# A spectral filter and a Fourier mixing layer on one core: a turn by DMAs or by TensorE, loads of x by halves or by groups, stores ordered or not

## The chip, the core and the metric

The kernel runs on one core of a Trainium2 chip. The metric is the device time in microseconds of one execution, median of several; shorter is better. A core has TensorE (matrix products; in the profile PE, its weight loads PEld), VectorE (DVE), ScalarE (ACT), GpSimd (POOL) and SyncE (SP), which here only issues loads. Each engine works through its own queue in order and waits on semaphores. 16 DMA engines move data between HBM and the on-chip memory SBUF, whatever engine issues the transfer. TensorE writes to PSUM, eight banks, from which ScalarE or VectorE must fetch the result.

## The reference

Two heads are computed from inputs of their own and set side by side.

```python
X = jnp.fft.rfft2(x_A, axes=(-2, -1))            # x_A: 1 x 2048 x 512
a = jnp.fft.irfft2(X * (w_r + 1j * w_i), s=(2048, 512), axes=(-2, -1))
p = jnp.einsum("bsd,ed->bse", x_B, dft_hid_re)   # x_B: 1 x 2048 x 512
q = jnp.einsum("bsd,ed->bse", x_B, dft_hid_im)
b = jnp.einsum("ts,bse->bte", dft_seq_re, p) - jnp.einsum("ts,bse->bte", dft_seq_im, q)
return jnp.concatenate([a, b], axis=-1)
```

Head A filters in the frequency domain. Head B is a two-dimensional Fourier transform, real part, whose transform matrices (2048 x 2048 and 512 x 512, cosine and sine) are inputs. All is float32.

## The kernel before, in words

The program is traced as named steps, and `PLAN` (lines 23 to 39) is the order in which they are written. Each step issues instructions on one engine or a few. Every instruction of TensorE, VectorE, ScalarE, GpSimd and SyncE goes through `_InOrder` (line 222), which pins it behind the one written before it on its engine; so each queue runs in the plan's order, and the profile shows the helper's line 229 for nearly all of them. They are told apart by tile names.

**Head A** splits the 2048 places of the sequence into 16 x 128.
- `forward(i)`, i = 0 to 7 (line 320): `xa` loads a slice of x transposed (tile `blk`), `fold` adds and subtracts its mirrored halves on VectorE (into `work`), `hid` applies the transform along the 512 channels (eight products of 256 columns, table `ta`, into a PSUM tile `pa`), `zs` copies to SBUF on ScalarE, `f16_` applies the 16-place transform (two products of 512 columns, the table f16 being the stationary operand), `ys` copies back. Then `tu` turns the data: two DMAs on POOL's queue write the result into eight partitions of the tile `zv` each, 16 DMAs in all, so that afterwards each partition holds one of 128 places.
- `slot(e, n)`, eight slots in the order `SLOTS` (line 386): `w` loads the filter's weights and a small table `fi`, `fix` (POOL) sets one column of the weights, `sf` (VectorE) folds z from `zv` into `work`, `fwd` is the 128-place transform (two products of 512 columns; slot 0 eight of 256), `prod` and `comb` multiply by the filter and combine on VectorE, `inv` transforms back (eight products of 128 columns), `ev` copies from PSUM to `zv` on ScalarE in two instructions. Slot 0, third in order, has special steps `g2`, `sx2`, `spec2`, `spy`.
- `inverse(j)` (line 513): `hi` is eight products of 256 columns that read `zv` with a stride as stationary operand, `eu` copies, `g16` is eight products of 128 columns, `sc` and `eo` add and subtract into `work`, and `st` stores 1 MB of out_a from POOL's queue after every second j. There are two places for what is stored; the third waits for the first one's store.

**Head B** uses that the given matrices are those of a Fourier transform, computes with small tables, and checks that they are.
- `xb` loads x by quarters (four tiles of 1 MB in the ring `blk`), each in two halves: rows going up on partitions 0 to 63 and rows going down on 64 to 127. The last half is loaded in three parts. `xr` reverses a part on ScalarE, `al` is four products on each of 16 groups (table `fb`), `av` copies to `yall`.
- `bh` is five products (table `bt`, with `yall` as stationary operand; the third has one row and 257 columns), `hv` copies to `zb`, `ro` is the product for one of eight blocks of rows. `y1`, `y2`, `y3` (ScalarE, VectorE, ScalarE) assemble 2 x 128 rows in a tile `yb`, of which there are two, and `pt` stores them from POOL's queue: a plain store (`out_b<-yb`) and an indirect one that writes the mirrored rows by an index table (`out_b<-yb,turn`). As both write the tensor out_b, each store waits for the one before it.
- The check: `cl` loads a block of the given matrices (1 MB, ring `blk`), `cc` compares it with a table `tt` on VectorE (SCALAR_TENSOR_TENSOR with a count of what differs); `sg` changes signs in the table on ScalarE. There are 34 blocks. If anything differs, a slow general path runs after the rest (it doesn't here).

The ring `blk` has six places of 1 MB for A's x, B's x and the matrices alike, given out in the order of the plan, and SP waits before a load until its place is free. PSUM has three tiles `pa` (head A, two banks each) and two `pb`.

Of the kernel before, what the change touches and what calls it, by code (L numbers as in the profile page):

```python
# [24 lines left out]
tu0 w1 f16_1 zs2 hid3 ys1 tu1 w2 cc0 f16_2 zs3 fold7 hid4 xb0 cc1 cl2 fix0 f16_3 zs4 ys2 hid5 tu2 xb1 cl3 fix1
ys3 tu3 f16_4 zs5 cl4 fix2 cl5 hid6 xr0 f16_5 zs6 cc2 al0 ys4 al1 av0 tu4 hid7 av1 cc3 f16_6 zs7 ys5 al2 sg4
tu5 f16_7 av2 cc4 al3 late cl6 av3 cc5 cl7 xr1 ys6 al4 ys7 tu6 al5 av4 tu7 al6 av5 cc6 al7 av6 cl8 av7 cl9 xb2
xb3 cc7 fwd2 sf0 sf1 tt2 cc8 cl10 cc9 fwd0 g2 fwd1 prod0 cl11 xr2 cl12 al8 prod1 w3 al9 cl13 av8 al10 av9
comb0 w4 al11 av10 av11 cl14 comb1 xr3 al12 sx2 al13 av12 cc10 al14 spec2 av13 inv0 av14 prod2 fix3 inv1 ev0
sf3 w5 al15 ev1 comb2 fwd3 cl15 av15 cl16 fix4 bh8 prod3 spy inv2 hv8 sf4 w6 fix5 comb3 fwd4 ev2 sf5 inv3  # L30
prod4 bh0 ev3 sf6 fix6 w7 fwd5 comb4 hv0 ro0 prod5 fix7 inv4 y10 y20 comb5 bh1 y30 ev4 rx sf7 hv1 fwd6 ry cc11
pt0 ro1 bh2 y11 prod6 cl17 sg12 inv5 hv2 y21 comb6 y31 ro2 ev5 pt1 bh3 y12 cc12 inv6 hv3 y22 cl18 fwd7 ev6
cc13 y32 ro3 pt2 bh4 prod7 y13 cl19 y23 hv4 comb7 ro4 y33 pt3 bh5 y14 cc14 inv7 hv5 y24 cl20 ev7 cc15 ro5 y34
bh6 y15 pt4 cc16 tt3 cl21 hi0 hv6 y25 cl22 sg17 y35 cc17 pt5 ro6 eu0 bh7 y16 tt4 cl23 y26 y36 g16_0 cc18 hv7
pt6 ro7 sc0 hi1 cc19 cl24 eo0 cl25 hi2 cc20 eu1 y17 y27 cl26 cc21 y37 g16_1 eu2 pt7 g16_2 cl27 sg22 sc1 cc22
hi3 sc2 eo1 cl28 eo2 st0 hi4 eu3 cc23 cc24 cl29 g16_3 eu4 g16_4 sc3 cc25 cl30 hi5 sc4 eo3 cl31 cc26 st1 hi6
eu5 cc27 cl32 eo4 cl33 eu6 cc28 g16_5 g16_6 sc5 cc29 hi7 sc6 eo5 sg30 cc30 st2 eu7 cc31 g16_7 eo6 sc7 eo7 cc32
st3 cc33
# [103 lines left out]
def _tables():  # L142
# [54 lines left out]
    for h in range(2):  # L197
        for kb in range(2):
            th = _ang(np.outer(_freqs(h), place[kb]), D)
            c, s = 2 * np.cos(th), -2 * np.sin(th)  # L200
            if h == 0:
# [18 lines left out]


class _InOrder:

    def __init__(self, tc, engine):
        self._tc, self._engine = tc, engine

    def __getattr__(self, name):
        def issue(*args, **kwargs):
            return self._tc.keep_in_program_order(getattr(self._engine, name)(*args, **kwargs))  # L229
# [4 lines left out]
def kernel(  # L234
# [85 lines left out]
    def forward(i):  # L320
        b, c = divmod(i, 2)
        zs = part(4096 + 1024 * (i % 2), 2, 512)
        ys = part(6144 + 1024 * (i % 2), 2, 512)
# [573 lines left out]
```

## Time and profile before

| | us |
|---|---|
| median of 3 runs | 258.09 (257.47 to 258.71) |
| the profiled execution, as timed | 258.96 |
| its span, first to last instruction | 257.2 |
| TensorE busy | 195.9 |
| VectorE busy | 154.0 |
| ScalarE busy | 71.9 |
| GpSimd busy | 39.3 |
| bytes moved | 70.35 MB, of these 57.54 read from HBM and 8.39 written |
| mean granted clock of TensorE | 0.856 of full speed |

Busy time of TensorE is modelled from pipelined products, so a full TensorE need not be at its peak. An idle time is printed with what ended it. The last instructions are the check's sum and its flag; after them the span holds 5.2 us without work.

### The profile page before, as it was taken

How to read it: one execution, taken by the hardware profiler on the slowest of the kernel's cores; microseconds unless marked ns; L12 is line 12 of the kernel's file. 1: busy time of each engine (PE TensorE's matmuls, PEld its weight loads, DVE VectorE, ACT ScalarE, POOL GpSimd, SP SyncE). 2: the span in 40 equal slices, each digit the busy share in tenths (PEclk: the TensorE clock that was granted, in tenths of full speed). 3: DMA queues.
4: the chain of work that ended last, by engine and by line, in shares of the span. 5: the costliest groups of instructions: out<-in, count | busy, mean ns of one | idle time of the engine just before them, and what ended most of it. 6: DMA issues, size and time to landing. Idle time of an engine off the chain costs nothing. (4 is left out here: it accounts for less than half of the span.)

```text
span 257.2 us, 2443 instructions
## 1 busy us (share of the span) xinstructions
PE 195.9 (76%) x857; PEld 153.9 (60%) x857; DVE 154.0 (60%) x209; ACT 71.9 (28%) x114; POOL 39.3 (15%) x55
## 2 busy tenths in 40 slices
PE   6799999397470798979999946994939999906800
PEld 1577776385470667948667623772718999906700
DVE  0730550031573789999999937814057799408990
ACT  1034150421720034531255402314031623300300
POOL 3002131012120000221013112010121120700110
PEclk9799999889677599999999985696577999965975
DMA  6989999999999999997314581786659889992440
GB/s 246 413 364 414 395 402 240 291 241 389 399 397 318 212 240 402 413 371 265 106 43 149 166 294 52 253 291 267 169 240 327 316 299 357 360 410 95 163 162 12
DMA packets 21746, 70.35 MB, mean 274 GB/s; under 512 B 2896, under 2 KB 3792, under 8 KB 20832
## 3 DMA queue, kind: packets, MB, share of 16 engines
q1 hardware_dynamic: 16656, 56.33, 63.8%
q0 software_dynamic: 4928, 13.22, 14.2%
q10 hardware_dynamic: 144, 0.59, 0.7%
q8 instruction: 8, 0.13, 0.2%
q14 instruction: 10, 0.08, 0.1%
HBM read 57.54 MB, written 8.39 MB: 256 GB/s over the span
## 5 line engine op out<-in xcount | busy, mean ns | idle before, releaser
L229 PE MATMUL pa<-ta,work 128*128 128x256 f32 (+1 forms) x256 | 48.8, 352 | 12.7 <-DVE work L229 11.5
L229 PEld LDWEIGHTS pa<-ta,work 128*128 128x128 f32 x256 | 43.3, 211 | 20.1 <-issue 10.2
L229 ACT COPY work<-pa 128x1024 f32<-128x1024 f32 (+3 forms) x36 | 30.4, 859 | 85.1 <-PE pa L229 82.9
L229 DVE SCALAR_TENSOR_TENSOR blk<-blk,tt 128x2048 f32<-128x2048 f32 (+2 forms) x24 | 41.6, 1756 | 20.3 <-DMA blk<-in_cm 17.4
L229 DVE SCALAR_TENSOR_TENSOR blk<-blk,odd,tt 128x2048 f32<-128x2048 f32 x16 | 37.5, 2346 | 21.7 <-DMA blk<-in_cm 21.7
L229 PE MATMUL pa<-ta,zv 128*128 128x256 f32 x128 | 31.0, 402 | 0.0
L229 PEld LDWEIGHTS pa<-ta,zv 128*128 128x128 f32 x128 | 29.7, 307 | 1.8 <-issue 1.0
L229 PE MATMUL pb<-bt,yall 128*128 128x257 f32 (+2 forms) x90 | 29.1, 459 | 0.0
L229 PEld LDWEIGHTS pb<-bt,yall 128*128 128x128 f32 (+1 forms) x90 | 18.0, 219 | 13.2 <-issue 11.7
L229 PE MATMUL pb<-fb,blk 128*128 128x200 f32 (+1 forms) x64 | 17.3, 358 | 8.3 <-ACT yall L229 4.4
L229 PE MATMUL pb<-zb,bt 128*128 128x512 f32 (+3 forms) x24 | 12.8, 641 | 13.8 <-ACT zb L229 13.8
L229 DVE TENSOR_TENSOR yb<-yb,pb 128x255 f32<-128x255 f32 x16 | 6.0, 415 | 26.4 <-ACT yb L229 26.4
L229 DVE TENSOR_TENSOR work<-work 128x512 f32<-128x512 f32 x32 | 20.6, 687 | 0.3
L229 PEld LDWEIGHTS pb<-fb,blk 128*128 128x128 f32 x64 | 13.2, 226 | 10.8 <-issue 5.9
L229 PE MATMUL pb<-fb,xr 128*128 128x200 f32 (+1 forms) x64 | 17.5, 359 | 2.1 <-ACT xr L229 2.1
L229 PEld LDWEIGHTS pa<-fi,work 128*128 128x128 f32 x144 | 18.6, 205 | 0.9 <-issue 0.5
L229 PE MATMUL pa<-fi,work 128*128 128x128 f32 x144 | 18.5, 288 | 0.0
L229 POOL DMA_INDIRECT out_b<-yb,turn x8 | 13.5, 1688 | 30.5 <-DMA out_b<-yb 16.9
L229 DVE TENSOR_TENSOR work<-pa,work 128x512 f32<-128x512 f32 x18 | 11.4, 682 | 11.2 <-DMA out_a<-work 11.2
L229 DVE TENSOR_TENSOR work<-pa,w 128x1024 f32<-128x1024 f32 x14 | 16.4, 1219 | 0.8 <-PE pa L229 0.8
L229 POOL DMA_DIRECT2D zv<-work x16 | 9.6, 605 | 46.8 <-ACT work L229 46.4
L229 ACT COPY yb<-pb 128x514 f32<-128x514 f32 (+1 forms) x9 | 5.1, 565 | 36.8 <-DMA out_b<-yb,turn 23.9
(48 smaller groups left out, 157.6 us busy)
## 6 DMA issues: line engine op xcount, KB each, us to landing
blk<-in_cm SPq DMA_DIRECT2D x32, 1024.0 KB, 10.7
tt<-tab_tt SPq DMA_DIRECT2D x4, 1026.0 KB, 10.5
w<-in_wa SPq DMA_DIRECT2D x8, 512.0 KB, 12.6
zv<-work POOLq DMA_DIRECT2D x16, 256.0 KB, 9.0
out_a<-work POOLq DMA_DIRECT2D x4, 1024.0 KB, 7.4
blk<-in_xb SPq DMA_DIRECT2D x7, 512.0 KB, 18.4
blk<-in_xa SPq DMA_DIRECT2D x4, 512.0 KB, 6.9
blk<-in_xa SPq DMA_DIRECT2D x2, 1024.0 KB, 11.0
```

Of the source, the lines that this page charges most:

```text
L229: return self._tc.keep_in_program_order(getattr(self._engine, name)(*args, **kwargs))
```

## The change

*A's turn.* `f16_` now takes the data as stationary operand, in eight pieces of 128 x 128, and the 16-place table as moving one: eight products of 128 columns in place of two of 512, with the result turned. `ys` writes it with a stride into a tile `fz`, so that the 128 places of a slot's rows lie in 128 consecutive columns. The step `tu` with its 16 DMAs is gone. Each slot gets two new steps instead: `tr` (eight, PE transposes of 128 x 128 against an identity matrix `eye`, which POOL loads at the start) and `ez` (ScalarE copies to SBUF, half of the result for seven slots, all of it for slot 0). `sf` reads one operand from PSUM and one from SBUF. `ev` is one copy, and `hi` reads `fz` with another stride. `fix` is now a copy on VectorE within `prod`. `m` in `work` has one place instead of two.

*x of B.* The load is by 16 groups of 64 + 64 rows, 256 KB each: one DMA for all 128 partitions of a group (three for the last), whose source has two runs of 64 rows as outermost dimension. `xr` still takes a quarter, four groups.

*out_b.* The stores are declared independent of each other. Every third block is assembled in `work` instead of in one of the two tiles `yb`, so three can be in flight.

*Besides.* `bh`'s third product takes every second column (128 instead of 257). The order of the queues is held by another means, which leaves out POOL: its instructions are ordered by the library's scheduler. `PLAN` is new throughout, and the numbers of the compared blocks (`cl`, `cc`, `sg`) have changed. The core of the diff:

```diff
-xa0 we xa1 xa2 xa3 xa5 xa7 tt0 tt1 bt fold0 cl0 fold1 hid0 cl1 fb fold3 hid1 zs0 w0 f16_0 zs1 fold5 hid2 ys0
...
+xa0 we xa1 xa2 xa3 xa5 xa7 cl0 cl1 fb fold0 hid0 bt fold1 tt0 cl2 fold3 hid1 zs0 cl3 tt1 f16_0 zs1 fold5 hid2
+ys0 cl4 f16_1 zs2 w0 hid3 ys1 f16_2 zs3 fold7 w1 hid4 ys2 cc0 xb0 cc1 f16_3 zs4 xb1 hid5 cc2 ys3 xb2 cc3 f16_4
+zs5 xb3 cc4 sg0 hid6 ys4 cl5 cl6 cl7 cl8 xb4 f16_5 zs6 xb5 xb6 hid7 xb7 xr0 ys5 cc5 f16_6 zs7 f16_7 w2 cc6 ys6
+al0 ys7 late cc7 al1 av0 tr0 av1 tr1 sg1 cc8 tr2 ez0 ez1 al2 sf0 al3 av2 sf1 fwd0 xb8 av3 xb9 xb10 xb11 cl9
+cl10 xr1 cl11 cl12 fwd1 prod0 ez2 fwd2 comb0 w3 prod1 tr3 g2 al4 ez3 al5 comb1 av4 w4 inv0 av5 sx2 al6 ev0 sf3
+al7 spec2 av6 cc9 cl13 inv1 av7 xr2 tr4 ev1 prod2 fwd3 ez4 comb2 al8 w5 al9 av8 al10 sf4 av9 spy al11 cc10
+av10 inv2 xb12 av11 xb13 xb14 xb15 cl14 prod3 cl15 fwd4 ev2 comb3 w6 tr5 xr3 tr6 prod4 ez5 al12 ez6 al13 av12
...
+st0 cc22 y36 pt6 cc23 cl28 ro7 eu2 hi3 y17 cc24 cl29 y27 g16_2 cl30 eu3 cc25 y37 g16_3 sc2 pt7 eo2 cl31 sg4
...
-    pe, dve, act, pool, sync = (_InOrder(tc, e) for e in (nc.tensor, nc.vector, nc.scalar, nc.gpsimd, nc.sync))
+    pe, dve, act, pool, sync = nc.tensor, nc.vector, nc.scalar, nc.gpsimd, nc.sync
...
+    written.enter_context(tc.manual_schedule(engines={e.engine for e in (pe, dve, act, sync)}))
...
-    zv = const("zv", 16, 512)
+    fz = const("fz", 4, 16, 128)
...
+    eye = const("eye", P, src=tabs["first"][:, 1152:], by=pool)
...
         @step(f"f16_{i}")
         def _():
-            y = flat(bank_a(("py", i)))
+            y = bank_a(("py", i)).rearrange("p r h q f -> p r (h q) f")
             for r in range(2):
-                mm(y[:, r], f16, zs[:, r], start=True, stop=True)
+                for c in range(4):
+                    mm(y[:, r, c], zs[:, r, 128 * c : 128 * c + 128], f16, start=True, stop=True)
...
-            act.copy(ys, flat(at["py", i]))
-
-        @step(f"tu{i}")
-        def _():
-            for r in range(2):
-                lo = _place(8 * r + i, 0)
-                pool.dma_start(zv[lo : lo + 29 : 4], ys[:, r])
+            act.copy(fz.rearrange("p c k (n g) -> p g (c k n)", g=16)[:, i::8], flat(at["py", i]))
...
-        m = part(3072 + 2048 * (n % 2), 2, 2, 4, 128)
+        m = part(3072, 2, 2, 4, 128)
+        z = part(5120 + (512 * (n % 2) if e else 0), 1 if e else 2, 2, 2, 128)
...
-        @step(f"fix{n}")
-        def _():
-            pool.tensor_copy(at["w", n][:, 0, :, :, 0], we[:, e].rearrange("p f r -> p r f"))
...
+        @step(f"tr{n}")
+        def _():
+            pz = bank_a(("pz", n)).rearrange("p r h q f -> p r (h q) f")
+            for r in range(2):
+                for c in range(4):
+                    pe.transpose(pz[:, r, c], fz[:, c, 2 * e + r], eye)
+
+        @step(f"ez{n}")
+        def _():
+            act.copy(z, at["pz", n][:, :1] if e else at["pz", n])
...
-                TT(out=t[:, :, 0], in0=z[:, 1], in1=z[:, 0, :, ::-1], op=ADD)
-                TT(out=t[:, :, 1], in0=z[:, 0], in1=z[:, 1, :, ::-1], op=SUB)
-                dve.tensor_copy(t[:, 0, :, :, 0], z[:, :, 0, :, 0])
+                pz = at["pz", n]
+                TT(out=t[:, :, 0], in0=pz[:, 1], in1=z[:, 0, :, ::-1], op=ADD)
+                TT(out=t[:, :, 1], in0=z[:, 0], in1=pz[:, 1, :, ::-1], op=SUB)
+                dve.tensor_copy(t[:, 0, :, :, 0], pz[:, :, 0, :, 0])
...
             x, w = at["px", n] if e else t, at["w", n]
+            dve.tensor_copy(w[:, 0, :, :, 0], we[:, e].rearrange("p f r -> p r f"))
...
-            for i in range(2):
-                act.copy(zv[:, 2 * e + i].rearrange("p (n q g) -> p n q g", n=8, q=4),
-                         at["pi", n][:, i].rearrange("p q h (n g) -> p n (q h) g", n=8))
+            act.copy(fz[:, :, 2 * e : 2 * e + 2].rearrange("p c k f -> p k c f"),
+                     at["pi", n].rearrange("p k h q f -> p k (h q) f"))
...
-                        mm(pu[:, k, h], gz[:, 32 * q + 16 * h + 2 * j + k :: 64], at["di"][:, h, q],
+                        mm(pu[:, k, h], gz[:, 2 * h + q, 2 * j + k], at["di"][:, h, q],
...
-            x = at["x", q] = block(("xb", q)).rearrange("p (g d) -> p g d", g=4)
-            lo = 16 + 256 * q
-            load(x[:64], src[lo : lo + 256].rearrange("(g r) d -> r g d", r=64))
-            lo = 16 * 124 - 256 * q - 192
-            if q < 3:
-                load(x[64:], src[lo : lo + 256].rearrange("(g r) d -> r g d", r=64)[:, ::-1])
...
+                if g == 0:
+                    at["x", q] = block(("xb", q)).rearrange("p (g d) -> p g d", g=4)
+                x, lo, low = at["x", q], 16 + 64 * n, 1984 - 64 * n
+                if n < 15:
+                    load(x[:, g], bass.AP(xb.tensor, lo * D, [[(low - lo) * D, 2], [D, 64], [1, D]]))
+                else:
+                    load(x[:64, g], src[lo : lo + 64])
+                    load(x[64:80, g], src[:16])
+                    load(x[80:, g], src[low + 16 : low + 64])
...
-            mm(out, yall[0:1, 9 + a1], hc[0:1, 1], start=False, stop=True)
+            mm(out[:, 1::2], yall[0:1, 9 + a1], hc[0:1, 1, 1::2], start=False, stop=True)
...
-            y = at["y", o] = sp.tile([P, 2, 512], F32, name="yb", bufs=2)
+            y = at["y", o] = sp.tile([P, 2, 512], F32, name="yb", bufs=2) if o % 3 < 2 else part(7168, 2, 512)
...
+                stores = [pool.dma_start(rows[8 * k, :64], y[64 * k : 64 * k + 64, 0]) for k in range(2)]
+            to = bass.IndirectOffsetOnAxis(ap=turn[:, o : o + 1], axis=0)
+            stores.append(pool.indirect_dma_start(out=out_b, out_offset=to, in_=y[:, 1], in_offset=None))
+            for i in stores:
+                tc.declare_no_dep(i.ins, group="rows", reason="every store has rows of its own")
+                tc.add_to_no_dep_group("rows", i.ins)
```

More of the change, by code (lines that the diff above doesn't have):

```diff
@@ L23 @@
 PLAN = """
-xa0 we xa1 xa2 xa3 xa5 xa7 tt0 tt1 bt fold0 cl0 fold1 hid0 cl1 fb fold3 hid1 zs0 w0 f16_0 zs1 fold5 hid2 ys0
[L25 to L38, printed above, removed]
+xa0 we xa1 xa2 xa3 xa5 xa7 cl0 cl1 fb fold0 hid0 bt fold1 tt0 cl2 fold3 hid1 zs0 cl3 tt1 f16_0 zs1 fold5 hid2
@@ new lines @@
+av10 inv2 xb12 av11 xb13 xb14 xb15 cl14 prod3 cl15 fwd4 ev2 comb3 w6 tr5 xr3 tr6 prod4 ez5 al12 ez6 al13 av12
+comb4 inv3 av13 sf5 al14 w7 ev3 al15 sf6 av14 inv4 av15 cc11 fwd5 ev4 cc12 cl16 tt2 fwd6 prod5 cl17 tr7 bh8
+ez7 comb5 bh0 hv8 prod6 inv5 hv0 ro0 comb6 ev5 bh1 y10 sf7 y20 inv6 hv1 cc13 y30 fwd7 ev6 cc14 cl18 cl19 rx
+ro1 ry prod7 y11 cl20 bh2 pt0 comb7 hv2 y21 inv7 cc15 y31 pt1 ro2 ev7 bh3 cc16 cl21 tt3 y12 hi0 hv3 y22 cl22
+sg2 y32 cc17 pt2 ro3 eu0 bh4 cl23 tt4 y13 y23 g16_0 y33 hv4 pt3 ro4 sc0 bh5 eo0 y14 y24 hi1 cc18 hv5 y34 pt4
@@ L206, in _tables @@
     first = np.concatenate([hf.reshape(2, 128, 512).transpose(1, 0, 2).reshape(128, 1024),
-                            f16.transpose(0, 1, 3, 2).reshape(128, 128)], 1)
+                            f16.reshape(128, 128), np.eye(128)], 1)
     late = np.concatenate([di.reshape(128, 1024), g16], 1)
@@ L483, in _ @@
         def _():
-            pi, it = bank_a(("pi", n)).rearrange("p r q h f -> p r (q h) f"), at["it", n]
+            pi, it = bank_a(("pi", n)).rearrange("p r h q f -> p r (h q) f"), at["it", n]
             for i in range(2):
                 for q in range(4):
-                    lhs = [yo[:, q % 2, k, q // 2] for k in range(2)]
+                    lhs = [yo[:, q // 2, k, q % 2] for k in range(2)]
                     if e:
@@ L681, in _ @@
             if o:
-                pool.dma_start(rows[o], y[:, 0])
+                stores = [pool.dma_start(rows[o], y[:, 0])]
             else:
-                for k in range(2):
-                    pool.dma_start(rows[8 * k, :64], y[64 * k : 64 * k + 64, 0])
-            pool.indirect_dma_start(out=out_b, out_offset=bass.IndirectOffsetOnAxis(ap=turn[:, o : o + 1], axis=0),
-                                    in_=y[:, 1], in_offset=None)
+                stores = [pool.dma_start(rows[8 * k, :64], y[64 * k : 64 * k + 64, 0]) for k in range(2)]
[4 more added lines that the diff above has]
+                tc.add_to_no_dep_group("rows", i.ins)
     for e in range(9):
@@ L760 @@
         table(k, q, mt)
-        for j in range(2 if q is None else 8):
-            if q is None:
-                compare_hidden(16 + j, j)
-            else:
-                i = 8 * k + j - (6 if k > 2 else 0)
-                compare(i, k, q, mt, *divmod(j, 4))
+        if q is None:
+            for h in range(2):
+                compare_hidden(16 + h, h)
+        else:
+            for j in range(8):
+                half, tb = divmod(j, 4)
+                compare(18 * q + 8 * half + 4 * mt + tb, k, q, mt, half, tb)
     for name in PLAN.split():
@@ L776 @@
     dve.tensor_scalar(flag, pf, 0.0, None, op0=ALU.is_equal)
+    written.close()
     first.close()
```

35 lines of the change are left out of this document (15 added, 20 removed).

## The prediction

> **What bounds the kernel now.** I read the totals first, then the stretches of the span, the chain of waits, the waits by engine, and the timeline around the two places that the chain pointed to.
>
> ```profile
> span 257.2 us, 2443 instructions
> PE 195.9 (76%) x857; PEld 153.9 (60%) x857; DVE 154.0 (60%) x209; ACT 71.9 (28%) x114; POOL 39.3 (15%) x55
> DMA packets 21746, 70.35 MB, mean 274 GB/s; under 512 B 2896, under 2 KB 3792, under 8 KB 20832
> ```
>
> No engine fills the span: TensorE has 61 us without work, VectorE 103. The time is in stretches with different limits (columns: stretch, its length, busy us of PE, PEld, DVE, ACT, POOL with instructions, granted clock, DMA share, GB/s):
>
> ```profile
> 0.00:43.60 43.60, 39.40 (x143) 27.99 (x144) 14.76 (x19) 11.31 (x11) 7.55 (x20) 0.96 0.96 356
> 43.60:93.40 49.80, 31.14 (x112) 24.52 (x111) 21.28 (x22) 13.40 (x22) 5.36 (x9) 0.79 1.05 312
> 93.40:150.00 56.60, 54.04 (x290) 40.67 (x289) 55.93 (x83) 22.98 (x46) 10.06 (x10) 1.00 0.69 244
> 150.00:200.00 50.00, 36.16 (x113) 26.44 (x113) 23.17 (x43) 11.29 (x20) 7.04 (x9) 0.69 0.66 236
> 200.00:222.50 22.50, 22.50 (x134) 22.45 (x134) 20.07 (x22) 8.02 (x10) 6.58 (x4) 1.00 0.90 331
> 222.50:233.00 10.50, 2.70 (x21) 2.48 (x19) 0.58 (x1) 1.60 (x2) 1.18 (x2) 0.73 0.99 378
> 233.00:252.00 19.00, 9.92 (x50) 9.38 (x50) 18.20 (x22) 3.33 (x4) 1.51 (x2) 0.77 0.30 115
> ```
>
> Up to 43.6 TensorE is the limit: A's hidden transform and 16-place transform follow each other without a gap. From 43.6 to 93.4 nothing computes fully while the DMA engines are full. From 93.4 to 150, A's slots keep VectorE at 99% and TensorE at 95%. From 150 on there are holes of 27 us (150 to 200) and 10 us (222.5 to 233) in VectorE. The first weak stretch in the timeline:
>
> ```profile
> 39.31 3.62 PE L229 MATMUL pa<-ta,work 128*128 128x256 f32 x16
> 42.77 1.88 PE L229 MATMUL pa<-work,ta 128*128 128x512 f32 x4
> 48.52 1.14 ACT L229 COPY xr<-blk 128x4 f32<-128x4 f32 x2 [9.65 <-DMA blk<-in_xb]
> 53.48 3.62 PE L229 MATMUL pa<-ta,work 128*128 128x256 f32 x16
> 68.47 1.94 ACT L229 COPY work<-pa 128x1024 f32<-128x1024 f32 x2
> 69.78 2.40 POOL L229 DMA_DIRECT2D zv<-work  x4 [7.20 <-ACT work L229]
> 85.13 6.46 PE L229 MATMUL pa<-zv,fi 128*128 128x256 f32 x16 [9.45 <-issue]
> 93.41 4.62 DVE L229 TENSOR_TENSOR work<-pa,w 128x1024 f32<-128x1024 f32 x4 [0.83 <-PE pa L229]
> ```
>
> Step hid6 starts at 39.31 and hid7 only at 53.48: ScalarE stands 9.65 us at xr0 for x of B, and zs6 behind it would have freed hid7's bank. Then the last two turns, tu6 and tu7, are issued at 69.78, and the first slot starts when they have landed, at 85.1. How transfers fared there:
>
> ```profile
> 20.00:30.00 10.00, 10.00 (x40) 7.33 (x39) 1.22 (x1) 3.04 (x3) 2.46 (x4) 1.00 1.02 407
> 80.00:90.00 10.00, 4.87 (x12) 3.91 (x13) 4.73 (x7) 0.00 (x0) 0.00 (x0) 0.52 1.07 230
> 90.00:100.00 10.00, 10.00 (x48) 7.58 (x46) 9.13 (x12) 3.34 (x7) 0.00 (x0) 0.96 1.04 296
> zv<-work POOLq DMA_DIRECT2D x16, 256.0 KB, 9.0
> blk<-in_xb SPq DMA_DIRECT2D x7, 512.0 KB, 18.4
> ```
>
> With equal DMA share (1.02 to 1.07) the engines moved 407 GB/s at 20 to 30 and 230 to 296 at 80 to 100, where the loads of x on 64 partitions lie. So these loads hold the engines without using them.
>
> The late holes, in the chain of waits and the waits by engine:
>
> ```profile
> 168.31 7.78 DMA out_b<-yb,turn
> 176.64 2.94 DMA out_b<-yb
> 180.35 8.08 DMA out_b<-yb,turn
> 222.14 10.18 DMA out_a<-work
> ACT yb L229 <- DMA out_b<-yb,turn: 23.9, 4, 9.2
> POOL out_b L229 <- DMA out_b<-yb: 16.9, 5, 5.5
> DVE yb L229 <- ACT yb L229: 26.4, 5, 8.9
> DVE work L229 <- DMA out_a<-work: 11.2, 1, 11.2
> ```
>
> The stores of out_b run one behind the other: a block's plain store, then its indirect one, then the next block's, 12.0 us a block (168.31 to 180.35). y1 waits for its buffer on ScalarE, y2 stands behind it on VectorE, and the compares, whose releases let SP load further blocks, stand behind y2.
>
> **The change, part by part.** Durations of the work it changes (the row with 4.66 is a stretch of TensorE's products with fb alone, four steps al; the row with slashes gives shortest, median and longest ns, first and last start):
>
> ```profile
> 120.41 1.95 PE L229 MATMUL pa<-fi,work 128*128 128x128 f32 x16
> L229 PE MATMUL pa<-work,ta 128*128 128x512 f32 x32 | 15.0, 593 | 0.0
> L229 ACT COPY zv<-pa 128x512 f32<-128x512 f32 x16 | 8.5, 585 | 9.5 <-PE pa L229 9.5
> L229 DVE COPY work<-zv 128x4 f32<-128x4 f32 x7 | 1.2, 171 | 0.2
> L229 PE MATMUL pb<-bt,yall 1*128 1x257 f32 x18 | 7.3, 490 | 0.0
> 94.86:99.52 4.66, 4.66 (x32) 4.66 (x32) 1.00 1.01 372
> L229 POOL DMA_INDIRECT out_b<-yb,turn x8: 1005/1326/2998, 135.7 to 219.1; - x8
> out_a<-work POOLq DMA_DIRECT2D x4, 1024.0 KB, 7.4
> SPq L229 <- DVE blk L229: 99.4, 22, 13.4
> ```
>
> *The 16-place transform* becomes eight products of 128 columns per i in place of two of 512. Eight products of that size with their weight loads took 1.95 us (inv, 120.41), against 1.88 us for the two: 8 x 0.07 = 0.6 us more, on TensorE's path.
>
> *The turn.* Sixteen DMAs of 256 KB go, with 4.2 MB of traffic and their wait: from the end of ys7 (70.4) to 85.1 it is 14.7 us. In their place stand 64 PE transposes and eight copies ez. No transpose is in this trace. The nearest row is the 128-column product, 1.95 / 8 = 0.24 us. The lower bound is half of it, if a transpose makes one pass where a product makes two (each product shows as two instructions); the upper is twice it, at half clock: 8, 16 or 31 us. I take 0.24, the row of the same shapes: 15.6 us, of which 5.9 lie before the first product. The Trainium skill, TensorE: Matmul & The Clock Gate, "Part 4: PE-mode transpose", gives some 275 ns for a bf16 transpose inside a kernel; by that figure the 64 would be an estimated 17.6 us and the sum 2 us more, and no run here shows it. The copies ez (0.59 us, 1.0 for slot 0) lie on ScalarE, 28% busy; only the first, 0.6 us, is on the path. ys writes with a stride: between 1.0 us as now and 2 us; up to 1 us on the path, since ScalarE has 5.4 us per i for two copies. ev loses one of two issues, nothing. sf reads one operand from PSUM; products of pa and w on the same engine do too, so I add nothing.
>
> *fix* goes from POOL to VectorE: 8 x 0.17 = 1.4 us on the path of the slots.
>
> *x by groups.* 18 issues on SP instead of 10, some 0.4 us each, 3 us, hidden under SP's 99 us of waiting for blocks; without that cover they are 3 us. If the groups move at the full 407 GB/s, the two stretches that held x lose their loss: 80 to 100 carried 5.3 MB where 8.1 would fit (7 us), 40 to 60 about as much. Behind SP's x loads are queued the cosine blocks, for which VectorE waits; behind xr on ScalarE everything that A needs there.
>
> *bh's third product* takes every second column: half of 7.3 us, 3.6 us off TensorE at most, 2 at full clock; I take 2. The eye load (64 KB, POOL) is long landed when tr0 starts.
>
> *out_b unordered, a third yb.* A buffer is held for about 2 us of y1 to y3, the issues, and 8 us of landing, 12 us; with three, one block per 4 us can go. TensorE's pace per block (bh and ro) is slower than that where hi and g16 lie between, so the wait goes. POOL is no longer held in written order, and st0 stands before pt6 and pt7 in the new order, so the 11.2 us wait for out_a's buffer shrinks; I leave 3 us of it.
>
> **The sum.** The slots' first product stands at 93.41 now. In the new order TensorE's chain sets it: f16_0 follows hid1 at 17 us as now and ends at 19, then six pairs of hid and f16 at 5.5 us (33 us), f16_7 to 54, ys7 to 55.3, al0, al1, tr0 to tr2, al2, al3, fwd0 to 67. By then x0 is there: 15.4 MB are ahead of it in SP's order (4.2 of A, five cosine blocks 5.2, tables 4.6, w 1.3, by the sizes of the loads), at 0.4 MB/us from 2 us 41 us, landed at 45. So the first product comes at **67**, 26 us earlier.
>
> From there TensorE is the longest. Its busy time from 93.4 on is 54.0 + 36.2 + 22.5 + 2.7 + 9.9 = 125.3 us. Moved behind the point: al4 to al7, 4.7; fwd1 and fwd2 (two products of 512 and eight of 256, as f16 and hid above), 5.5; tr3 to tr7, 9.8; less 2 for bh: 143. Of it 36.2 us ran at a clock of 0.69, 2.7 at 0.73 and 9.9 at 0.77; at 1.0, as where TensorE has no holes, they would take up to 14 us less. I take 10.5: 132.5. TensorE's share in the dense stretch 93.4 to 150 was 95%, so 139.5 us: the last product ends at 206.5. VectorE from the same point has 118.0 us as now, one compare (2.3) and fix (1.4) more, 121.7, which fits beneath; DMA has 66 MB, 165 us at 0.4, which fits too. After the last product come eo and st3: 1.3 + 0.8 + 7.4 landing, about 10; 3 us for out_a's buffer: 219.5. The profiled execution lies 1.8 us above its span (258.96 to 257.2): 221.3 on its scale, where the median of the runs is 0.9 lower: **220**. Its own range is 209 to 232: transposes at half price (8 us less) and a clock of 1.0 throughout (3.5 less) give the low end; transposes at twice the price, of whose 15.6 us VectorE's work covers a part, the high one.
>
> **The rivals.**
>
> *A: a group of x moves on two DMA engines only; slower.* The new source has two runs of 64 rows as its outermost dimension. If the transfer is divided over the engines by that count, each of two engines gets 128 KB per group. At 407/16 = 25.4 GB/s that is 5.2 us per group and 77 us for fifteen, on engines whose equal share of the other 62 MB is already 152 us: 229 us at the least. Worse, all later loads queue behind: x0 to x3 end at 62, four cosine blocks at 2.6 us and x4 to x7 at 93, w2 and x8 to x11 at 117, four blocks, w and x12 to x15 at 152. Each xr holds ScalarE until then. After 152 TensorE still has al12 to al15, four slots' second half, bh, ro and all of hi and g16, some 92 us by the rows above (al 4.7, inv 9.8, tr 2, the wider products by their columns at hid's 3.62 us for 2048), at 95% 97; with 13 us of tail and out_a's buffer, and 0.9 to the median's scale, **263**. It decides from two engines up to about four (a group 2.6 us: 245). For it: the shape. Against: in this trace all loads on SP had 64 or 128 rows outermost, so it shows neither. The Trainium skill, DMA: Bandwidth & Descriptors, "Why a DMA increments its semaphore by 16 and not by 1", says that the slowest dimension of both sides sets the number of engines, the largest up to 16 that divides both, which here would be two. No row here shows it; by that rule this rival is the result.
>
> *B: TensorE runs slow.* If the holes between short transposes keep the clock at its mean of 0.86, 143 stays 143: 150.5 at 95%, 11 us more than above, **231**. For it: 0.69 to 0.79 wherever TensorE waited. The Trainium skill, TensorE: Matmul & The Clock Gate, says in the section named above that transposes do not release the clock gate as products do; no row here has one.
>
> *C: the stores still pace.* From the first indirect store at 135.7 to the end of the last one's issue at 222.1 it is 86.4 us. Starting 26 us earlier but at that pace, with the 35 us that lie behind it now: 231.2, **232** with what lies around the span. That the change doesn't do what it says lies here: an order kept by another semaphore, or by POOL's own. Against it: no store reads what another writes.
>
> **Chances.** The forecast has 0.43, A 0.36 (slower 0.31, within 0.5% 0.03, faster 0.02), B 0.12, C 0.07, others 0.02 divided evenly. Faster by over 0.5% (about what this measurement tells from nothing): 0.43 + 0.02 + 0.12 + 0.07 + 0.01 = 0.65; same 0.03; slower 0.32. The range goes from 209 to 269: it cuts a tenth of the forecast and a quarter of A.
>
> **What would show it.** First product at 67 and xr0 before 50; 230 to 296 GB/s at full DMA share gone; transposes of 0.24 us; no wait of ScalarE for out_b's stores over 3 us. It is wrong if a group of x lands later than 10 us after issue, if xr1 to xr3 wait, or if the late clock stays under 0.8.

## The result, and the profile after

The change made the kernel slower: 275.51 us (274.81 to 275.87) against 257.78 us (257.14 to 258.71) for the kernel before, measured beside it, a ratio of 1.068 with a 95% interval of 1.064 to 1.072. The forecast was 220 us; rival A had 263.

The totals of the changed kernel:

```profile
span 273.2 us, 2751 instructions
PE 188.9 (69%) x1017; PEld 161.7 (59%) x1017; DVE 156.3 (57%) x217; ACT 83.5 (31%) x114; POOL 22.5 (8%) x32
GB/s 253 406 409 410 421 370 57 82 302 282 89 85 51 178 50 52 115 294 371 324 51 52 228 247 102 176 379 4 324 193 343 421 379 380 419 420 420 387 55 117
```

TensorE has 7 us less to do than before and POOL 17 us less, and the span is 16 us longer. The last of the three lines gives the moved bytes in 40 slices: in the middle it falls again and again to 50 to 57 GB/s, and once to 4. The same in stretches of 10 us (columns as in the prediction's table of stretches; the second last is the share of 16 DMA engines):

```profile
20.00:30.00 10.00, 10.00 (x62) 9.17 (x62) 1.88 (x3) 5.57 (x4) 0.00 (x0) 1.00 1.01 411
100.00:110.00 10.00, 8.78 (x37) 7.61 (x38) 1.34 (x3) 2.39 (x4) 0.00 (x0) 0.68 0.14 52
140.00:150.00 10.00, 10.00 (x69) 9.08 (x68) 5.08 (x8) 3.73 (x9) 0.00 (x0) 0.98 0.14 52
```

A share of 0.14 of sixteen engines is 2.2 engines, and they move 52 GB/s: two engines at 26 GB/s each, with the other 14 as good as idle. The loads of x on SP's queue (shortest, median and longest ns, first and last start):

```profile
L581 SPq DMA_DIRECT2D blk<-in_xb x15: 543/5062/11112, 31.7 to 140.1; - x15
```

and in the kernel before:

```profile
L229 SPq DMA_DIRECT2D blk<-in_xb x10: 596/631/1758, 32.8 to 80.2; - x10
```

SP stands 5.06 us at a group in the median, which is as long as 256 KB take at 52 GB/s (262,144 bytes / 52 = 5.04 us). What that does to the loads behind it shows in the timeline of SP's queue, loads of one kind in a row put together:

```profile
31.73 15.76 SPq L581 DMA_DIRECT2D blk<-in_xb  x4
47.60 10.62 SPq L712 DMA_DIRECT2D blk<-in_cm  x4
58.32 25.18 SPq L581 DMA_DIRECT2D blk<-in_xb  x4
83.53 5.12 SPq L387 DMA_DIRECT2D w<-in_wa  x1
88.69 0.47 SPq L260 DMA_DIRECT2D fi<-tab_fi  x1
89.26 18.84 SPq L581 DMA_DIRECT2D blk<-in_xb  x4
```

The six rows add up to 76.0 of the 76.4 us from 31.7 to 108.1; short gaps between the loads of a row are in them (1.8 us in the first), and by the single issues SP stands for 73.6. The weights and tables for A's slots, which the plan puts between the groups, go out when the groups before them have been taken. Who waits for all this:

```profile
ACT xr L594 <- DMA blk<-in_xb: 47.5, 3, 19.1
DVE blk L700 <- DMA blk<-in_cm: 40.2, 4, 25.5
PE pa L423 <- DMA fi<-tab_fi: 20.1, 1, 20.1
PE pa L427 <- DMA fi<-tab_fi: 18.0, 1, 18.0
POOL out_b L681 <- ACT yb L663: 18.8, 5, 5.0
```

ScalarE waits 47.5 us for x (before it was 9.65 at xr0 and next to nothing later), and TensorE 20.1 for one small table of 128 KB and 18.0 for that of slot 0, 512 KB. VectorE's 40.2 for the matrices are no more than before (39.1). The last line answers to the stores of out_b: POOL now waits for the block to be assembled, and no engine waits for a store. The places in time:

```profile
65.04 0.20 ACT L594 COPY xr<-blk 128x4 f32<-128x4 f32 x1 [19.07 <-DMA blk<-in_xb]
81.53 2.35 DVE L458 TENSOR_TENSOR work<-pa,w 128x1024 f32<-128x1024 f32 x2 [1.44 <-PE pa L423]
98.72 0.20 ACT L594 COPY xr<-blk 128x4 f32<-128x4 f32 x1 [18.46 <-DMA blk<-in_xb]
125.32 0.20 ACT L594 COPY xr<-blk 128x4 f32<-128x4 f32 x1 [10.01 <-DMA blk<-in_xb]
163.07 0.20 ACT L594 COPY xr<-blk 128x4 f32<-128x4 f32 x1 [12.86 <-DMA fi<-tab_fi]
```

The four quarters of x are copied at 65, 99, 125 and 163, and the first product of slots stands at 81.5 instead of 67. The last row puts its wait down to a table, but releasers are inferred and `xr` reads nothing but x: with that row ScalarE's waits before xr are 60.4 us. After the last quarter the kernel runs as it was meant to:

```profile
81.50:163.00 81.50, 33.38 (x190) 27.58 (x189) 34.84 (x52) 13.41 (x26) 0.00 (x0) 0.72 0.53 168
200.00:262.00 62.00, 61.91 (x329) 55.80 (x328) 52.82 (x74) 25.28 (x38) 16.48 (x17) 0.98 0.93 365
```

From 81.5 to 163 TensorE worked 41% of the time, from 200 on 100% at a clock of 0.98.

### The profile page after: what moved, and what is told of

It is laid out like the page before. It is cut to its first block, busy times and chain, and to the rows that moved or that the text cites. A ratio compares the mean times of both kernels' runs of the same rounds, so it can differ in the third digit from the quotient of the medians.

```text
span 273.2 us, 2751 instructions
## 1 busy us (share of the span) xinstructions
PE 188.9 (69%) x1017; PEld 161.7 (59%) x1017; DVE 156.3 (57%) x217; ACT 83.5 (31%) x114; POOL 22.5 (8%) x32
## 2 busy tenths in 40 slices
DMA packets 19393, 66.24 MB, mean 242 GB/s; under 512 B 1550, under 2 KB 2446, under 8 KB 18478
## 4 chain that ended last, share of the span: by engine, by line
DMA 33%; PE 32%; SPq 21%; DVE 9%; ACT 2%; issue 1%; ACTq 0%; DVEq 0%
SPq L581 14%; PE pa L519 10%; DMA blk<-in_cm 8%; DMA fi<-tab_fi 8%; DMA w<-in_wa 7%; DMA blk<-in_xb 6%; PE pa L531 5%; SPq L712 4%; DMA blk<-in_xa 4%; PE pa L484 3%; DVE work L458 3%; DVE blk L700 2%; PE pa L427 2%; PE pb L631 2%; PE pb L643 2%; SPq L387 2%
## 5 line engine op out<-in xcount | busy, mean ns | idle before, releaser
L346 PE MATMUL pa<-ta,work 128*128 128x256 f32 x128 | 31.5, 404 | 3.5 <-DVE work L334 3.5
L346 PEld LDWEIGHTS pa<-ta,work 128*128 128x128 f32 x128 | 25.6, 204 | 8.2 <-DVE work L334 4.4
L519 PE MATMUL pa<-ta,fz 128*128 128x256 f32 x128 | 29.5, 386 | 0.0
L519 PEld LDWEIGHTS pa<-ta,fz 128*128 128x128 f32 x128 | 28.9, 305 | 0.4 <-issue 0.2
L358 PE MATMUL pa<-ta,work 128*128 128x128 f32 x128 | 17.3, 293 | 17.0 <-ACT work L351 17.0
L423 PE MATMUL pa<-work,fi 128*128 128x512 f32 x28 | 14.4, 652 | 20.1 <-DMA fi<-tab_fi 20.1
L358 PEld LDWEIGHTS pa<-ta,work 128*128 128x128 f32 x128 | 17.0, 209 | 17.5 <-ACT work L351 17.2
L606 PE MATMUL pb<-fb,xr 128*128 128x200 f32 (+1 forms) x64 | 15.8, 330 | 11.3 <-ACT xr L595 11.3
L423 PEld LDWEIGHTS pa<-work,fi 128*128 128x128 f32 x28 | 5.4, 209 | 25.2 <-DVE work L416 20.3
L594 ACT COPY xr<-blk 128x4 f32<-128x4 f32 x4 | 0.8, 198 | 60.4 <-DMA blk<-in_xb 47.5
L606 PEld LDWEIGHTS pb<-fb,xr 128*128 128x128 f32 x64 | 11.5, 204 | 11.6 <-ACT xr L595 11.6
L362 ACT COPY fz<-pa 128x1024 f32<-128x1024 f32 x8 | 15.4, 1931 | 4.8 <-PE pa L358 4.8
L427 PEld LDWEIGHTS pa<-work,fi 128*128 128x128 f32 x16 | 4.7, 304 | 19.9 <-ACT work L408 18.8
L531 PEld LDWEIGHTS pa<-ta,work 128*128 128x128 f32 x128 | 15.1, 192 | 0.2
L351 ACT COPY work<-pa 128x1024 f32<-128x1024 f32 x8 | 8.1, 1018 | 22.9 <-PE pa L346 22.9
```

Of the source, the lines that this page charges most:

```text
L346: mm(pd[:, r, h], us(b)[:, h, c, k, 128 * r : 128 * r + 128], hf[:, k, h], start=k == 0, stop=k == 1)
L358: mm(y[:, r, c], zs[:, r, 128 * c : 128 * c + 128], f16, start=True, stop=True)
L362: act.copy(fz.rearrange("p c k (n g) -> p g (c k n)", g=16)[:, i::8], flat(at["py", i]))
L423: mm(flat(px[:, h]), ft[:, 0], flat(t[:, h]), start=True, stop=True)
L427: mm(px[:, h, i], ft[:, 2 * i + j], z[:, j, h], start=j == 0, stop=j == 1)
L519: mm(pu[:, k, h], gz[:, 2 * h + q, 2 * j + k], at["di"][:, h, q], start=q == 0, stop=q == 1)
```

## The experiments

Each run had runs of the kernel before beside it, whose medians were 256.7 to 259.5 us. "Laid out" means that the host puts the rows of x into the groups' order before the launch; that is no version for a user whose x comes in its own order, and its cost on the host is not in the time. All times are medians in us.

| kernel | time | ratio to before (interval) |
|---|---|---|
| before, with the two-run groups of x | 314.4 | 1.224 (1.217 to 1.231) |
| the change | 275.5 | 1.068 (1.064 to 1.072) |
| before, x laid out | 247.9 | 0.953 (0.945 to 0.962) |
| the change, groups with 4 outermost | 243.0 | 0.940 (0.930 to 0.950) |
| the change, groups by POOL's queue | 235.3 | 0.906 (0.899 to 0.913) |
| before, stores unordered | 226.4 | 0.878 (0.871 to 0.886) |
| the change, groups with 8 outermost | 220.7 | 0.855 (0.847 to 0.863) |
| the change, one group in four with two runs | 220.3 | 0.853 (0.848 to 0.857) |
| the change, x laid out, stores ordered | 218.1 | 0.845 (0.837 to 0.853) |
| before, x laid out, stores unordered | 215.9 | 0.830 (0.824 to 0.836) |
| the change, each group as two loads | 209.7 | 0.809 (0.801 to 0.817) |
| the change, x laid out | 205.3 | 0.796 (0.788 to 0.803) |

**Theory: a group of x moves on two engines, since two runs are the outermost dimension of its source, and everything behind it is late. Rival: the groups are a symptom; the new order, the transposes or the clock cost the time.** The first two runs take the two-run source away: once by laying out the rows, so that 128 rows are outermost, and once by two loads of 64 rows.

```diff
-load(x[:, g], bass.AP(xb.tensor, lo * D, [[(low - lo) * D, 2], [D, 64], [1, D]]))
+load(x[:, g], xg[:, n])
```

> The changed kernel with one thing else: the rows of x of B lie in HBM in the order in which the groups want them (a second copy of the input in another layout), so that each group is one load whose source has 128 rows outermost, 256 KB as before, 16 loads in all. Nothing else differs. Theory 1 (two engines): the source with two runs of 64 rows was divided over two DMA engines, and that alone turned a gain into a loss; then no stretch has under 60 GB/s with SP issuing x, the waits of ScalarE for x (47.5 us) fall under 5 us, the first product of the slots stands at 65 to 75 us instead of 81.5, and the time is 220, between 212 and 230. Rival (the new order and the work on TensorE and ScalarE cost the time, the loads are only where it shows): 255 to 275.

Measured: 204.9 us (204.3 to 206.1). Here the laid-out rows came in another order than the groups need, so its out_b was that of permuted rows; loads and instructions are the same. With the right rows:

```diff
+rows_b = np.concatenate([16 + 64 * np.arange(16) + np.arange(64)[:, None], low + np.arange(64)[:, None]])
+rows_b[64:80, 15] = np.arange(16)
+xg = xb.reshape(2048, 512)[rows_b]
```

> As the run with the laid-out rows, but with the rows taken in the order that the groups of the reference's sum need (in the earlier run they were taken from the input in another order, so its out_b was that of permuted rows; sizes and transfers were the same). The time should not see it: 205, between 203 and 208.

Measured: 205.3 us (204.1 to 206.9). Nothing but these loads was changed, their shape and the place of their rows (the three loads of the last group are one here), and 70.2 us went. The loads on SP's queue in this kernel:

```profile
L581 SPq DMA_DIRECT2D blk<-in_xg x16: 327/374/1983, 31.3 to 82.6; - x16
```

SP is held 0.37 us for a group instead of 5.06 (medians). The rival falls: the order and the transposes are the same here, and the clock went from 0.857 to 0.961 by itself once the holes were gone.

```diff
-load(x[:, g], bass.AP(xb.tensor, lo * D, [[(low - lo) * D, 2], [D, 64], [1, D]]))
+load(x[:64, g], src[lo : lo + 64])
+load(x[64:, g], src[low : low + 64])
```

> The changed kernel with each group of x loaded by two loads of 64 partitions instead of one of 128 (33 issues on SP instead of 18). Theory 1: every load has 64 rows outermost and goes over all engines, at the reduced rate that the kernel before had for 64 partitions (230 to 296 GB/s); 4 MB of that cost at most 10 us against the laid-out rows, most of it hidden: 220 to 234. Rival (SP's many issues are what holds the queue, 5 us each): with nearly twice the issues it is no faster than the changed kernel, 270 to 290.

Measured: 209.7 us (206.8 to 210.8), a ratio of 0.809 to the kernel before, with x as the user has it and nearly twice the loads: 65.8 us less than with one load a group. Laid-out rows have 0.796. The Trainium skill, DMA: Bandwidth & Descriptors, "Rules for kernel authors", advises one load of 128 partitions over two to disjoint halves. The medians of these two runs differ that way, by 4.4 us, but the intervals of their ratios overlap, so the runs don't settle it; and the merged load of the change is one load of 128 partitions as well.

**The groups alone, on the kernel before.**

```diff
-            load(x[:64], src[lo : lo + 256].rearrange("(g r) d -> r g d", r=64))
...
+            for g in range(4):
...
+                    load(x[:, g], bass.AP(xb.tensor, lo * D, [[(low - lo) * D, 2], [D, 64], [1, D]]))
```

> The kernel before with the new load of x alone: four groups, each one load whose source has two runs of 64 rows, in place of two loads of 64 partitions per quarter; order, turn by DMAs and ordered stores as before. Theory 1: each group takes some 5 us on two engines and SP, 16 of them; the four quarters' xr come 15 to 40 us later than before, and the time is 280, between 270 and 300. Rival (the damage is in the new order): 255 to 262.

Measured: 314.4 us (313.5 to 315.2), 57.6 more than the kernel before beside it.

```profile
L229 SPq DMA_DIRECT2D blk<-in_xb x18: 414/5088/8583, 32.8 to 144.5; - x18
```

SP's 5.09 us a group stand here too, with none of the rest of the change. So this part does the harm by itself; the rest of the change takes 38.9 us off again (314.4 to 275.5).

**Does the count of the outermost dimension set the number of engines?** The laid-out rows are padded, so that the source has 4 or 8 blocks outermost with the rest of the kernel as in the run with x laid out; the eight-block kernel has `[[272*D, 8], [16 * D, 16], [1, D]]`.

```diff
-load(x[:, g], xg[:, n])
+load(x[:, g], bass.AP(xg.tensor, n * D, [[528*D, 4], [16 * D, 32], [1, D]]))
```

> The laid-out rows, but stored in four runs of 32 rows with a gap behind each, so that the source of a group has 4 as its outermost dimension; same bytes, same number of loads, right rows. If the outermost count sets the number of DMA engines, a group takes 64 KB on each of four engines, 2.6 us at the 25 GB/s an engine had; SP's issue of a group takes about 2.5 us instead of 5; the four engines carry 40 us of x besides their share of the rest, and the time is 216, between 210 and 232. If only the two far runs of the changed kernel were special, it is 205.

> The same with eight runs of 16 rows. By the count: 32 KB on each of eight engines, 1.3 us a group, an issue about 1.3 us; nearly all hidden: 207, between 204 and 212, and not above the run with four. If the count means nothing, 205.

Measured: 243.0 us (241.1 to 243.3) and 220.7 us (220.2 to 221.1), both slower than expected. With four blocks, SP's queue, and a stretch in which SP issues only groups of x:

```profile
L581 SPq DMA_DIRECT2D blk<-in_xg x16: 529/2344/6946, 31.6 to 111.9; - x16
```

```profile
60.00:64.00 4.00, 3.76 (x17) 3.76 (x18) 3.70 (x5) 2.04 (x2) 0.00 (x0) 0.50 0.25 102
```

A share of 0.25 is four engines, at 25.5 GB/s each. So for two and four blocks the count is the number of engines, and SP's 2.34 us follow the 2.57 us that a group takes at 102 GB/s. With eight blocks SP is held 0.63 us, half of what the expectation had:

```profile
L581 SPq DMA_DIRECT2D blk<-in_xg x16: 596/633/3537, 31.9 to 95.5; - x16
```

The Trainium skill's rule, cited in the prediction under A (DMA: Bandwidth & Descriptors, "Why a DMA increments its semaphore by 16 and not by 1"), agrees with the traces for two and four. For eight no stretch shows the engines of a group: in the one in the last section blocks of the matrices are under way as well.

The size was missed because I had let most of each group's time lie beside other transfers. Worked out afterwards without any such cover, each load costs what it takes longer than the 0.64 us of 256 KB at 407 GB/s: 15 x (5.04 - 0.64) = 66 us for two, 16 x (2.57 - 0.64) = 31 for four, and with half of 2.57 as an estimate, 16 x 0.64 = 10 for eight. Measured against 205.3 us: 70, 38 and 15, each 4 to 7 us more than the sum. So other transfers cover hardly any of a group's time; where the 4 to 7 us come from was not followed, and for eight the rate is not shown by a run.

**Is it the loads themselves, or SP's standing?** One group in four is loaded by two runs, the three behind it are laid out.

```diff
+if g == 0:
+    load(x[:, g], bass.AP(xb.tensor, lo * D, [[(low - lo) * D, 2], [D, 64], [1, D]]))
+else:
     load(x[:, g], xg[:, n])
```

> The changed kernel with laid-out rows for x, but the first group of each of the four quarters is loaded as in the changed kernel (outermost dimension two), so four of sixteen loads go to two engines, with three full loads behind each. Theory one, that SP is held only once the two engines' backlog is deep: a lone group is taken at 0.5 to 0.7 us and its 5 us of moving lie beside the full loads behind it, 205 to 213 us. Theory two, that every such group costs the kernel what it cost on average in the changed kernel, (275.5 - 205.3) / 15 = 4.7 us, wherever it stands: 219 to 229 us, with SP held about 5 us for each.

Measured: 220.3 us (219.3 to 220.4 in five executions; a sixth took 651.6 us, for a reason that is not on record), in the time of theory two, 15.0 us for four such groups (the sum above gives 4 x 4.4 = 17.6). But theory one was right on SP's row, and neither saw the next:

```profile
L582 SPq DMA_DIRECT2D blk<-in_xb x4: 532/738/3048, 31.4 to 92.1; - x4
L584 SPq DMA_DIRECT2D blk<-in_xg x12: 328/608/7673, 33.8 to 96.9; - x12
```

The two-run groups are taken at 0.74 us in the median (one at 3.05); it is at the laid-out groups behind them that SP stands, up to 7.67 us. So the load at which SP stands need not be the one with the two runs: a load with 128 rows outermost is held too when a two-run group went out before it. What part of the chip makes it wait is not in the records.

```diff
-load(x[:, g], bass.AP(xb.tensor, lo * D, [[(low - lo) * D, 2], [D, 64], [1, D]]))
+pool.dma_start(x[:, g], bass.AP(xb.tensor, lo * D, [[(low - lo) * D, 2], [D, 64], [1, D]]))
```

> The changed kernel, and its fifteen two-row group loads of x are issued by POOL's queue in place of SP's; the groups and their access patterns stay as they are. Theory one, that the harm is SP being held: SP was held 5 us by each group, so that the loads behind it started late. With POOL held instead, SP's other loads go out at 0.4 to 0.6 us each, the first product of slots comes near 67 us, and the time is 225 to 245 us; some of the loss stays, since each group still takes 5 us (256 KB at 52 GB/s). Theory two, that the harm is the two engines themselves: every other load is spread over all the engines and so has parts behind the groups on those two, whoever issues them. Then the windows stay near 52 GB/s while groups move, loads other than x land 15 us or more after their issue, and the time is 262 to 282 us.

Measured: 235.3 us (234.8 to 235.8). The time is theory one's, but the run doesn't tell the two theories apart, for POOL's queue moves the same source in another way. Its rows of queues (packets, MB, share of the DMA engines), with those of the changed kernel behind them:

```profile
q0 software_dynamic: 10576, 13.07, 19.4%
```

```profile
q0 software_dynamic: 2656, 9.08, 8.7%
```

The fifteen groups are 7920 packets there, 528 each, most of them small (8480 packets under 512 bytes in this kernel, 1550 in the changed one), and the engines are all busy (a stretch of 10 us of the kernel with POOL's groups):

```profile
50.00:60.00 10.00, 1.23 (x11) 1.03 (x10) 3.51 (x3) 0.00 (x0) 2.28 (x3) 0.67 1.05 268
```

Whether one group is spread over all the engines there, or the next group takes other ones, is not in the records. So the idle engines and most of SP's standing (up to 4.30 us at a block of the matrices is left) went away together; how much each alone would cost stays open. The first product came at 83 us, not at 67 as expected: the four groups of x's first quarter were issued from 30.3 to 33.6 and copied at 66.4.

```profile
30.31 3.24 POOL L581 DMA_DIRECT2D blk<-in_xb  x4 [26.61 <-DVE work L337]
blk<-in_xb POOLq DMA_DIRECT2D x15, 256.0 KB, 27.2
```

A group takes 27.2 us from issue to landing here, in the median; the later ones also went out late, since POOL waited for places in the ring.

**What the rest is worth.** Four runs set A's new turn, with the new order and all else that goes with it (the third buffer, bh's third product), against the order of the stores. Stores ordered in the changed kernel, stores unordered in the kernel before (two buffers `yb` there):

```diff
 # the change, x laid out, stores ordered
-for i in stores:
-    tc.declare_no_dep(i.ins, group="rows", reason="every store has rows of its own")
-    tc.add_to_no_dep_group("rows", i.ins)
```

> The laid-out rows with out_b's stores left in order as in the kernel before; three buffers as in the changed kernel. If the order of the stores is worth as much here as in the kernel before (30 us), 230 to 240, with ScalarE or GpSimd waiting for the indirect stores; if the third buffer and the new order of the steps hide it, 206 to 214.

> The kernel before with the stores of out_b declared independent, two buffers yb as before, all else unchanged. If the stores' order made the holes between 150 and 200 us (27 us in VectorE), the blocks of rows follow at 5 to 8 us instead of 12, ScalarE's waits for the indirect stores (23.9 us) fall under 10, and the time is 238, between 230 and 246. If the two buffers are the limit, or the holes belong to the cosine blocks that SP loads, it is 250 to 258.

```diff
 # before, x laid out (and, in the second kernel, those three lines added)
-            load(x[:64], src[lo : lo + 256].rearrange("(g r) d -> r g d", r=64))
...
+            for g in range(4):
+                load(x[:, g], xg[:, 4 * q + g])
```

> The kernel before, with x read by sixteen groups from rows laid out in the groups' order (128 rows outermost in each load), and nothing else changed. Theory: x was not on the path in the kernel before (the copies xr waited 0.5 us for it), so full-rate groups bring at most the 2 us of the earlier row group: 252 to 259 us, a ratio of 0.98 to 1.00. Rival: that finer groups of x also let the transforms along x start earlier and fill TensorE's idle time: 235 to 248 us.

> The kernel before with the laid-out groups of x, and with the stores of out_b declared independent and two buffers yb; A's turn stays with its DMAs and the moving data. Against the changed kernel with laid-out rows (205.3 us) it shows what A's new turn and the order that goes with it are worth. Theory, that the parts add: 226.4 us of the stores alone less 0 to 3 us for x, 222 to 228 us, so that the turn is worth 17 to 23 us. Rival, that x and the stores together do nearly all of it: 205 to 213 us, and the turn is worth less than 8 us.

Measured, all with x laid out:

| | stores ordered | stores unordered | |
|---|---|---|---|
| A's turn by DMAs, the old order | 247.9 | 215.9 | -32.0 |
| the change: A's turn by transposes, the new order | 218.1 | 205.3 | -12.7 |
| | -29.8 | -10.6 | |

Three of the four runs fit neither of the ranges that their expectation gave. Ordered stores in the changed kernel gave 218.1, between the two. Unordered stores in the kernel before gave 226.4 us, 30.3 less than the kernel before beside it, more than expected. Together with x laid out they gave 215.9, between the two ranges. x laid out alone gave 247.9, 11.6 less, at the edge of what the rival had; the expectation had left out the 9.65 us that ScalarE waits at xr0. The two parts add there (30.3 + 11.6 = 41.9, measured 259.5 - 215.9 = 43.6). Turn and stores don't add: each gives some 30 us alone, and both together 42.5. So they go in part for the same time; which part that is, these runs don't show. The waits with ordered stores in the changed kernel:

```profile
ACT yb L648 <- DMA out_b<-yb,turn: 15.6, 2, 9.2
POOL out_b L677 <- DMA out_b<-yb,turn: 14.0, 3, 6.0
DVE yb L654 <- ACT yb L648: 11.3, 3, 7.6
ACT work L648 <- DMA out_b<-work,turn: 5.6, 1, 5.6
```

That is the chain of the kernel before (y1 for its buffer, y2 behind it), 15.6 us and, for the third buffer in `work`, 5.6 instead of 23.9, in spite of three buffers. Why x at full rate helps the kernel before, first as it was and then with x laid out, in the same 20 us:

```profile
30.00:50.00 20.00, 15.51 (x59) 10.90 (x59) 5.63 (x6) 5.44 (x7) 2.95 (x7) 0.99 1.05 324
```

```profile
30.00:50.00 20.00, 20.00 (x86) 15.41 (x85) 7.07 (x7) 7.65 (x11) 4.14 (x9) 1.00 1.05 394
```

TensorE has no hole there any more: ScalarE's wait at xr0 is 4.5 us instead of 9.65, and TensorE's stock of work covers it. These are 4.5 of the 11.6 us; where the others come from was not followed, nor whether the rate or the finer groups bring them.

## Why the prediction was wrong

**The step that failed** is "x by groups": "some 0.4 us each, 3 us, hidden under SP's 99 us of waiting" and "if the groups move at the full 407 GB/s". A group took 5.06 us of SP in the median and moved at 52 GB/s. Neither number had a row for this shape, and the text said so; the forecast took the rows of loads with 64 or 128 rows outermost for it. What could have been read in advance was read: A names the outermost dimension, the two engines and the order of what comes late, and the rule that would make it the result. I gave it 0.36 because no row showed it. But no row spoke against it either, and the forecast's own number hung as much on an unseen shape. The runs leave A as it was put, and they price it by itself: 70 us.

**A's size** was 263 against 275.5. It had the quarters of x at 62, 93, 117 and 152; they were copied at 65.0, 98.7, 125.3 and 163.1. So the lateness against A grows by some 3 us with each quarter (3.0, 5.7, 8.3, 11.1), and that is the miss, not the work behind it: from 163.1 to the end of the span it is 110.1 us, where A had 97 and 13. That this fits to 0.1 us is luck; the last products end at 261.9, so it is 98.8 and 11.3. Ahead of the fourth quarter SP stands at blocks and weights that were issued behind the third one's groups:

```profile
108.20 8.30 SPq L712 DMA_DIRECT2D blk<-in_cm  x4
116.60 4.18 SPq L387 DMA_DIRECT2D w<-in_wa  x1
135.84 9.31 SPq L581 DMA_DIRECT2D blk<-in_xb  x3
```

A had let every transfer follow the one before it without a gap, and had no term for SP's standing at an issue. How much of the 11 us each of the two makes was not followed further.

**With x at full rate the forecast was 15 us too high,** below its own range of 209 to 232. The kernel with x laid out, its transposes, its first product and its last products:

```profile
54.82 2.78 PE L405 MATMUL pa<-eye,fz 128*128 128x128 f32 x24
61.70 2.36 DVE L459 TENSOR_TENSOR work<-pa,w 128x1024 f32<-128x1024 f32 x2 [0.83 <-PE pa L424]
66.67 1.04 PE L405 MATMUL pa<-eye,fz 128*128 128x128 f32 x8
187.31 3.73 PE L532 MATMUL pa<-ta,work 128*128 128x128 f32 x32
```

- First product: forecast 67, measured 61.7. Of the 5.3 us, 3.1 are the first 24 transposes (5.9 forecast, 2.78 measured); 1.4 us more lie ahead of them, for the last 16-place product ends at 52.6 where the sum had 54. The remainder was not followed.
- From there to the last product of TensorE: forecast 139.5, measured 129.3 (61.7 to 191.0). The transposes are the largest term: eight take 1.04 us, 0.13 each, at the lower bound of 0.12, and each shows as one instruction, not two. I had taken the middle. For the 64 it is 7 us, 4.6 of them in this stretch (40 x 0.24 = 9.8, 40 x 0.13 = 5.2). Another 3.5 us would be the clock, if the 0.99 of the row under "The rivals" holds for the whole stretch: the sum had taken 10.5 of up to 14 us for a clock of 1.0.
- The tail: forecast 13 with 3 for out_a's buffer, measured 11.0 (191.0 to 202.0). No row of waits shows VectorE behind out_a's store any more. The three come to 17.5 us of the span; by the medians of the runs it is 15, since the profiled execution is the shortest of five.

**A duration at its upper bound, and off the path.** The strided ys, in the changed kernel, with the products whose result it copies and the next ones:

```profile
34.22 1.95 PE L358 MATMUL pa<-ta,work 128*128 128x128 f32 x16
36.20 1.97 ACT L362 COPY fz<-pa 128x1024 f32<-128x1024 f32 x1 [0.72 <-PE pa L358]
39.46 0.72 PE L358 MATMUL pa<-ta,work 128*128 128x128 f32 x5
```

It takes 1.97 us instead of 1.0, and the period of the pairs is 5.24 us (34.22 to 39.46; forecast 5.5), all of it TensorE's. So it costs nothing between the pairs, where the prediction had left up to 1 us on the path. The price of eight products in place of two, 1.95 us, was exact.

**The rivals.** B fell: with x laid out the clock from 65 to 185 us was 0.99, with the transposes in it.

```profile
65.00:185.00 120.00, 114.21 (x637) 97.74 (x636) 109.55 (x163) 49.15 (x81) 19.01 (x20) 0.99 0.85 320
```

TensorE's share there is 95%, the figure that the sum had used. What the Trainium skill says there of transposes and the clock (TensorE: Matmul & The Clock Gate, "Part 4: PE-mode transpose") made no difference that a run here shows: these transposes stand among products. C fell as well: no engine waits for a store of out_b in the changed kernel. But its subject was worth more than the sum gave it: with x laid out, ordering costs 12.7 us even in the new order, and 32.0 in the old one.

**By the signs named in advance:** "wrong if a group of x lands later than 10 us after issue, if xr1 to xr3 wait". xr waited 47.5 us (three of its four copies), and from 81.5 to 163 the clock was 0.72.

## What to carry to other kernels

Before a load is merged or reshaped, look at the outermost dimension of both its sides: if a small count comes to stand there (two, four and eight cost here), price the load at that many engines' rate, and count the difference for every such load in full, since the loads behind it on the queue wait too. Here one merged load a group cost 70 us over a layout with the partitions outermost; two loads with 64 rows outermost cost 4 by the medians, which is not clear of the noise. And when several parts of a change go for the same wait, run them singly: the stores alone, a few lines, brought the old kernel 30 us.

## What the runs showed of the hardware

- An engine that issues loads can stand at a load because of those before it: up to 7.67 us at groups with 128 rows outermost behind a two-run group, where the same loads took 0.37 us (median) and at most 1.98 with all of x laid out. Two-run groups are not the only cause: in the kernel before, without any, SP stood 7.25 us at one block of the matrices, issued behind x's loads to 64 partitions:

```profile
L229 SPq DMA_DIRECT2D blk<-in_cm x32: 367/368/7250, 7.7 to 221.3; - x32
```

- The transposes of float32 against an identity: 64 of them keep TensorE 7.8 us, 272 ns each from start to end (the end is modelled) but 109 ns from one start to the next. The 275 ns of the Trainium skill, TensorE: Matmul & The Clock Gate, "Part 4: PE-mode transpose", for bf16, agree with this duration; the distance of one from the next is two fifths of it:

```profile
L404 PE MATMUL pa<-eye,fz x64: 272/272/273, 74.7 to 178.2; 128*128 128x128 f32 x64
```

- A full share of the DMA engines is not the full rate. With eight blocks outermost, while groups and blocks of the matrices are under way:

```profile
72.00:76.00 4.00, 4.00 (x11) 3.23 (x12) 3.46 (x6) 0.00 (x0) 0.00 (x0) 0.58 1.05 218
```

All the engines count as busy and move 218 GB/s, where 411 were seen at a share of 1.01. The kernel before, with its loads of x to 64 partitions, had 324 at a share of 1.05, and 394 once x was laid out (the two rows from 30 to 50 us above). Why a load holds the engines longer than its bytes need was not tried.
